# GpSimd operations that wait for the VectorE operation ahead of them, one product split in two, one read moved from PSUM to SBUF, and a new order of the work

## The chip, the cores and the metric

The kernel runs on 1 core of one Trainium2 chip. The metric is the time of one execution on the device in microseconds (us), as the median of several runs. The core has five engines, which take their instructions in order, each from its own queue, and wait for each other by semaphores: TensorE (PE: matmuls; its weight loads are listed as PEld), VectorE (DVE), ScalarE (ACT: table functions such as Sin, Exp and Gelu, and copies), GpSimd (POOL), and SyncE (SP, which here issues DMAs).

## The reference

The input u has 2048 rows of 512 channels. It is normalised, passed through a long convolution whose kernel comes from a diagonal state-space model with 128 complex states for each channel, and added to itself; the result goes through two layernorms and an MLP of width 1376 and is added again. Cut to what matters:

```python
def conv(u):                                   # u: layernorm(x), [1, 2048, 512]
    dt = exp(log_dt)[:, None]
    logdA, dB = dt * (A_re + 1j*A_im), dt * (B_re + 1j*B_im)
    P = exp(logdA[:, :, None] * arange(L))
    K = einsum("dn,dnl,dn->dl", C_re + 1j*C_im, P, dB).real
    y = irfft(rfft(pad(u.T)) * rfft(pad(K)))[:, :L]       # causal, length 2L
    return y.T + u * Dskip

h  = x + conv(layernorm(x))
y  = layernorm(layernorm(h))
h2 = h + gelu(y @ w1 + b1) @ w2 + b2           # w1 512x1376, w2 1376x512
```

Inputs and the output are bf16.

## The kernel before

The kernel computes the convolution through a discrete Fourier transform that is written as matmuls. Its work comes in stages that overlap. First tables: dt, the phases and magnitudes of the states, the coefficients (names gr, gi, t4, den, HLq), small code tables (W2, W3, W4, S4, S2, codT, BD, DD) and the layernorm of the input (`bn_stats`, L913). They are made by DVE and ACT with the help of GpSimd. Parts of the phases are moved between partitions by 32 KB SBUF-to-SBUF DMAs on SP's queue, called restacks here (L541, `ar<-ar`). ACT also takes exponentials (L766).

Then comes the chain. A group of small matmuls (L1032, L1035, L1041) sums phase pieces in PSUM so that the low 16 bits of the result are an angle. ACT takes Sin of those 16 bits (L1050), once for the sine and once for the cosine. DVE multiplies a table of magnitudes with both. There are four such chains, B and A, each for hf=0 and hf=1. In a chain of kind A, and in the second half of a chain of kind B, one DVE operation of 128x2048 (`product`, recorded at L1011) writes the sine and the cosine part at once; in the first half of a B chain they are two operations of 1024 (L1061, L1063) with a negation between (L1062). Another Sin of 128x2048 (name T, L613) belongs to the phases that follow.

From the tables the matmuls of `kgen` (L1090, L1091) and of `kgen4` (L1121, L1122) make the convolution kernel. Four stages (0 to 3) of `kspec` (L1161) take it into frequency space; the stages 0 and 2 belong to the even lines. The result goes to DRAM and back in another layout (K0 and then K1; tiles AK_d), and `fstage` (L958) and `xspec` (L938, L958) finish the transforms of kernel and input. `inverse` multiplies the spectra (DVE, L1201), transforms back (PE, L1211) and transposes by DMA (`turn`, L1217). `tail(b, sb)` adds the residual (PE, L1275 and L1280), takes the statistics (`bn_stats`, L1288), normalises (L1303, L1305) and transposes (PE, L1313). `mlp` is the matmuls L1334 (w1, followed by Gelu on ACT, L1336) and L1356 (w2, followed by DVE, L1358) and the output's DMAs. w1 is loaded in four DMAs of 344 KB, w2 in three.

What sets the order: every operation is recorded with `add` as an entry with the engines it may run on and what it reads and writes. Its dependencies follow from that, by the byte ranges of the tiles. The list `ORDER` at the top names the entries in the order in which they are given out; a negative entry (the bitwise complement of the index) means the second of two engines. A helper `PD`, or `eng="POOL"`, makes an entry that may run on GpSimd or DVE; `CP` and `evac` one that may run on DVE or ACT. `Sched.run` walks the list with a model of costs. This model gives out the four PSUM tiles of 128x1024 f32, and it puts filler matmuls (L1450, results unused) where it expects TensorE to be idle for over 0.6 us; it moves no operation. At the end all operations are issued as listed, each engine's in the order of the list:

```python
    with tc.manual_schedule():
        for o in order:
            o.fn(o.e)
```

A wait is put in where an operation reads or writes bytes that another touches. GpSimd and DVE operations without common data have no order between them.

Of the kernel before, what the change touches and what calls it, by code (L numbers as in the profile page):

```python
# [15 lines left out]
P = 128  # L16
# [143 lines left out]
class VS(V):  # L160
# [93 lines left out]
class Sched:  # L254
# [42 lines left out]
    def run(self, nslots):  # L297
# [7 lines left out]
        slots = [0.0] * nslots  # L305
        taken = [None] * nslots
        dma_busy, bulk = 4.0, 4.0
        ipe, blk, md, pst, issued = 16, 0.0, 0, 0.0, 0.0
        order, seen = [], set()
        assert sorted(i if i >= 0 else ~i for i in ORDER) == list(range(len(ops)))  # L310
        for code in ORDER:
# [14 lines left out]
            if e == "DVE" and dv:  # L326
                s = max(s, pst)
# [75 lines left out]
def kernel(ctx, tc, A_u, A_A_re, A_A_im, A_B_re, A_B_im, A_C_re, A_C_im, A_log_dt, A_Dskip,  # L403
# [1054 lines left out]
    with tc.manual_schedule():  # L1458
        for o in order:
            o.fn(o.e)  # L1460
# [30 lines left out]
```

## Time and profile before

| what | us |
|---|---|
| median of 3 runs | 261.51 |
| lowest and highest run | 260.98, 262.74 |
| the profiled execution's own time | 261.88 |
| its span, first to last instruction | 260.0 |
| GpSimd's work after 43 us | 5.20 of 30.4 |

Times in the profile count from the start of the span. A group of instructions is named by its line in the code, the engine, the operation and what it writes and reads (`ar` is the SBUF arena, `ps` is PSUM), with the number of instructions, the busy time and the mean duration in ns. A row of a timeline gives start, duration and, in brackets, the idle time of the engine just before, with what ended it. Rows of queues end in q (SPq: a DMA issued by SP). The chain that ended last follows the work back from the last instruction, at each step to what released it.

### The profile page before, as it was taken

Reading aid. Unit: us, or ns where it says so; the run is one execution under the profiler, and the core shown is the slowest. Engines: PE = TensorE matmul, PEld = TensorE weight load, DVE = VectorE, ACT = ScalarE, POOL = GpSimd, SP = SyncE. Lnnn points to the kernel's source line nnn. Section 1 sums busy time; section 2 is a strip of 40 time slices with the busy share of each in tenths; the row PEclk is TensorE's granted clock in tenths of the full one; section 3 lists DMA queues with packets and bytes.
Section 4 is the critical chain, followed back from the end, with each engine's and each line's share of the span. In section 5 each row is a group of like instructions: output and inputs, shape, how many; then the busy total and the mean of one; then the engine's idle time right before and its main releaser. Section 6 shows DMA issues by size and latency. Waiting matters only on the chain.

```text
span 260.0 us, 7650 instructions
## 1 busy us (share of the span) xinstructions
PE 222.7 (86%) x3232; PEld 123.2 (47%) x3232; DVE 180.0 (69%) x352; ACT 175.9 (68%) x212; POOL 30.4 (12%) x212
## 2 busy tenths in 40 slices
PE   6307749976978999978999996899999999999994
PEld 2202523332756387423566863665544444444443
DVE  4699999699888858694899858676659962011022
ACT  2899968699978986886899946955620723623610
POOL 8665910070000000000000000000000000000000
PEclk9999995999999999997999999999999999999999
DMA  6981120110040142797476789714071051600302
GB/s 124 186 182 45 39 51 8 36 8 3 3 125 3 33 159 76 243 273 205 118 227 176 156 176 233 202 31 83 9 142 33 20 103 31 141 0 20 73 11 70
DMA packets 43203, 25.06 MB, mean 96 GB/s; under 512 B 27665, under 2 KB 40562, under 8 KB 43170
## 3 DMA queue, kind: packets, MB, share of 16 engines
q1 hardware_dynamic: 42578, 24.13, 38.6%
q10 hardware_dynamic: 592, 0.46, 1.2%
q8 instruction: 25, 0.41, 0.6%
q14 instruction: 8, 0.07, 0.1%
HBM read 10.03 MB, written 6.29 MB: 63 GB/s over the span
## 4 chain that ended last, share of the span: by engine, by line
PE 51%; ACT 15%; DMA 14%; DVE 10%; issue 4%; SPq 4%; ACTq 0%; DVEq 0%
PE ps L1334 15%; PE ps L1356 15%; ACT ar L529 7%; ACT ar L1050 6%; PE ps L1211 5%; DMA ar<-in_A_u_dram 5%; DMA ar<-ar 4%; SPq L541 3%; DMA ar<-AK_d 3%; PE ps L1450 3%; DMA AK_d<-ar 2%; DVE ar L606 2%; PE ps L1041 2%; DVE ar L1011 2%; PE ps L958 2%
## 5 line engine op out<-in xcount | busy, mean ns | idle before, releaser
L529 ACT CAST ar<-ps 128x1024 bf16<-128x1024 f32 (+4 forms) x74 | 66.7, 977 | 17.3 <-DVE ar L1288 5.9
L1336 ACT ACTIVATE ar<-ps,ar 128x512 bf16<-128x512 f32 (+1 forms) x44 | 28.8, 684 | 37.6 <-PE ps L1334 24.0
L1334 PE MATMUL ps<-ar 128*128 128x512 bf16 (+1 forms) x176 | 40.0, 379 | 0.0
L1356 PE MATMUL ps<-ar 128*128 128x512 bf16 (+3 forms) x187 | 39.9, 367 | 0.0
L1358 DVE TENSOR_TENSOR ar<-ps,ar 128x512 bf16<-128x512 f32 (+1 forms) x17 | 11.1, 659 | 40.4 <-PE ps L1356 29.8
L1050 ACT ACTIVATE ar<-ps 128x1024 bf16<-128x1024 int16 x36 | 34.9, 1053 | 4.1 <-PE ps L1041 2.8
L1201 DVE TENSOR_TENSOR ar<-ar 128x1024 bf16<-128x1024 bf16 x48 | 30.3, 686 | 10.2 <-PE ps L1211 9.7
L531 DVE CAST ar<-ps 128x1024 bf16<-128x1024 f32 (+3 forms) x26 | 28.5, 1116 | 9.4 <-PE ps L958 4.9
L1041 PE MATMUL ps<-ar 128*32 128x512 f16 (+1 forms) x368 | 23.5, 348 | 6.9 <-ACT ar L1050 3.7
L1356 PEld LDWEIGHTS <-ar 128*128 128x128 bf16 (+1 forms) x187 | 18.1, 98 | 20.0 <-issue 0.4
L1334 PEld LDWEIGHTS <-ar 128*128 128x128 bf16 (+1 forms) x176 | 17.4, 100 | 20.0
L1211 PE MATMUL ps<-ar 64*128 64x128 bf16 x768 | 24.0, 216 | 0.9 <-ACT ar L529 0.5
L1211 PEld LDWEIGHTS <-ar 64*128 64x128 bf16 x768 | 21.6, 94 | 6.3 <-DVE ar L1201 2.7
L1011 DVE TENSOR_TENSOR ar<-ar 128x2048 bf16<-128x2048 bf16 x18 | 21.7, 1222 | 3.1 <-PE ps L1091 2.6
L958 PE MATMUL ps<-ar 128*32 128x512 bf16 (+1 forms) x320 | 19.2, 363 | 4.9 <-ACT ar L529 2.4
L1450 PE MATMUL ps<-ar 128*128 128x512 bf16 x57 | 17.2, 450 | 5.7 <-DMA ar<-in_A_u_dram 5.1
L1041 PEld LDWEIGHTS <-ar 128*32 128x32 f16 x368 | 10.5, 101 | 17.7 <-issue 15.4
L613 ACT ACTIVATE ar<-ar 128x512 f32<-128x512 f32 (+9 forms) x19 | 12.6, 694 | 6.8 <-DVE ar L606 3.5
L766 ACT ACTIVATE ar<-ar 128x1024 bf16<-128x1024 f32 x16 | 15.7, 1042 | 0.8 <-DVE ar L600 0.8
L938 PE MATMUL ps<-ar 128*32 128x512 bf16 x256 | 15.4, 380 | 0.0
L606 DVE SCALAR_TENSOR_TENSOR ar<-ar 128x4 f32<-128x4 f32 (+4 forms) x44 | 13.3, 308 | 1.3 <-ACT ar L613 0.4
L958 PEld LDWEIGHTS <-ar 128*32 128x32 bf16 x320 | 8.2, 100 | 12.3 <-issue 6.4
(107 smaller groups left out, 281.0 us busy)
## 6 DMA issues: line engine op xcount, KB each, us to landing
ar<-AK_d SPq DMA_DIRECT2D x8, 512.0 KB
ar<-in_A_u_dram SPq DMA_DIRECT2D x4, 512.0 KB, 11.3
AK_d<-ar SPq DMA_DIRECT2D x2, 1024.0 KB
AK_d<-ar SPq DMA_DIRECT2D x4, 512.0 KB
out_dram<-ar SPq DMA_DIRECT2D x30, 64.0 KB, 2.0
ar<-in_B_w_dram SPq DMA_DIRECT2D x4, 344.0 KB, 6.8
ar<-ar SPq DMA_DIRECT2D x40, 32.0 KB, 1.8
ar<-in_B_w_dram SPq DMA_DIRECT2D x2, 640.0 KB
```

Of the source, the lines that this page charges most:

```text
L529: act.copy(out_fn(), in_fn())
L531: dve.tensor_copy(out_fn(), in_fn())
L958: pe.matmul(pst(p)[64 * h + z:64 * h + z + 32, w * (k + r):w * (k + r) + w], lhsT=T.ap()[:, f, r, z:z + 32], rhs=v[f:f + 1].ap()[:, 0, :], ...
L1011: dve.tensor_tensor(o, E_(o).unsqueeze(1).to_broadcast(shape), f, ALU.mult)
L1041: pe.matmul(pst(p)[32 * g:32 * g + 32, 256 * j:256 * (j + n)].rearrange("p (a b) -> p a b", a=n), lhsT=W2[DELTAS.index(d)].ap(), rhs=S2[g] ...
L1050: add("ACT", c_act(1024), lambda e, o_=o_, i_=i_: act.activation(o_(), i_(), ACT.Sin, scale=SINSC), r=[p, TBL], w=[sc[cs]])
L1201: dve.tensor_tensor(o, a, b_[:, :, ::-1, :] if sw else b_, ALU.mult)
L1211: pe.matmul(pst(p)[:, 512 * h + 128 * k:512 * h + 128 * k + 128], lhsT=q.ap()[rows, 2 * k + r, :], rhs=TP[w].ap()[rows, f0 // 2 + k, :], s ...
L1334: pe.matmul(pst(p)[:fs, 512 * z:512 * z + 512], lhsT=w1s[dc].ap()[:, fc * P:fc * P + fs], rhs=ybuf.ap().rearrange("p (t c) k -> p c t k", ...
L1336: add("ACT", c_act(512, 1), lambda e, p=p, z=z, fc=fc, fs=fs: act.activation(hT.ap()[:fs, fc, :], pst(p)[:fs, 512 * z:512 * z + 512], ACT. ...
L1356: pe.matmul(pst(p)[:, 512 * z + c0:512 * z + c1], lhsT=hT.ap()[:fs, fc, 128 * t:128 * t + 128], rhs=w2s[fc].ap()[:fs, c0:c1], start=(fc == ...
L1450: pe.matmul(slots[z][:, 0:512], lhsT=identb.ap(), rhs=hs[15].ap(), start=True, stop=True)
```

## The change

It has six parts.

1. `ORDER` is replaced by another list. Among the engines chosen by it: the product that makes W3 (128x640) and two memsets go from DVE to GpSimd; the product that makes W2, one conversion of 1024 for codT, the four conversions for DD (128x32) and one memset go from GpSimd to DVE; two conversions (th and the first half of HLq) go from DVE to ACT. The Sin of 128x2048 is listed during `kgen4`, not after the first two Sin of the chain. The kspec stages 0 and 2 come after the chain's last product, not ahead of it; the first 17 of 24 halves of `kgen4` precede all of `kspec`. 12 of the 16 pieces of the second `xspec` are listed ahead of the return of K0. The load of A_im stands second among SP's first loads, not behind two loads of u; the loads of u lie later, between restacks; that of B_re is issued on ACT's queue behind the one of log_dt. All four loads of w1 stand behind the fifth DMA transpose.
2. Every operation on GpSimd that is not a DMA waits for the last DVE instruction ahead of it in the list. `Sched.run` models this as `held`.
3. In the B chain with hf=1 the product of 2048 is written as two of 1024 (four products become eight).
4. The two copies of one transposed PSUM tile, crt (512, ACT) and cit (512, DVE), become one of 1024 on ACT.
5. In `tail(0, 0)` the copy from PSUM comes first, and `bn_stats` reads the copy.
6. The model's constants change: the first loads cost 1.25 times as much, a carry 0.75 and 57,344 B, a load of the spectrum 0.7, and fillers are put in from an idle time of 0.4 us on. There are 79 filler matmuls in place of 57; the other 3175 matmuls are the same in number.

Line numbers behind the changed parts are 4 to 15 higher in the kernel after (L1011 becomes L1015, L1050 becomes L1054, L1201 becomes L1209, L1450 becomes L1458).

```diff
 ORDER = [
-    182, 15, 0, 1, 12, 13, 16, 2, 311, 3, 5, 154, 17, 43, 37, 65, 66, 156, 18, 19, 4, 11, 20, 147, 36, 8, 67, 68, 21, 22, 23, 42, 44, 64, 45, 47, 57,
+    0, 1, 13, 143, 6, 2, 79, 12, 15, 144, 155, 3, 43, 110, 153, 11, 42, 80, 181, 4, -155, 32, 45, 5, 9, 44, -48, 16, 17, 59, 46, 14, 139, 65, 66, 60,
...
@@ Sched.run
+            if e == "POOL" and o.byts == 0:
+                s = max(s, held)
...
-            if e == "PE" and self.src <= seen and s - free[e] > 0.6 and fs:
+            if e == "PE" and self.src <= seen and s - free[e] > 0.4 and fs:
...
-                while t + (0.3 if clk.warm and clk.end > t else 0.55) < s and n0 < FILLN:
+                while t + (0.2 if clk.warm and clk.end > t else 0.4) < s and n0 < FILLN:
...
+            if e == "DVE":
+                held = end + LAG["DVE"]
...
-    crt, cit = tE(bf16, 512), tE(bf16, 512)
-    evac(by4(crt), pas[0], 512, [p], [crt])
-    evac(by4(cit), pas[1], 512, [p], [cit], pr=0.401)
+    cc = tE(bf16, 2, 512)
+    crt, cit = cc[0], cc[1]
+    evac(lambda: cc.ap().rearrange("p z (q d) -> p z q d", d=4), lambda p=p: pst(p, bf16)[:, 0:1024].rearrange("p (z d q) -> p z q d", z=2, d=4), 1024, [p], [cc])
...
             rE, rI = regs(e0, q, lo, 4), regs(i0, q, lo, 4)
+            if hf:
+                add("DVE", c_dve(1024, 2), lambda e, lo=lo, Sx=Sx, e0=e0, i0=i0, q=q: dve.tensor_tensor(ent(i0, q, lo, 4), ent(e0, q, lo, 4), Sx(), ALU.mult), r=rE + [sc[0]], w=rI)
+                add("DVE", c_dve(1024, 2), lambda e, lo=lo, Cx=Cx, e0=e0, q=q: dve.tensor_tensor(ent(e0, q, lo, 4), ent(e0, q, lo, 4), Cx(), ALU.mult), r=rE + [sc[1]], w=rE + mark)
+                continue
             product(lambda e0=e0, q=q, lo=lo: both(e0, q, lo, 4), lambda o: o[:, 1], sc, rE + [sc], rE + rI + mark)
...
-                add("DVE", c_dve(512, 1, True) + 0.05, lambda e, src=src, j=j, hh=hh: dve.bn_stats(st2[8 * b + j].ap(), src() if first else hh.ap()), r=[p if first else hh], w=[st2[8 * b + j]], hv=0)
-                if first:
+                else:
                     evac(lambda hh=hh: hh.ap(), src, 512, [p], [hh])
+                add("DVE", c_dve(512) + 0.05, lambda e, j=j, hh=hh: dve.bn_stats(st2[8 * b + j].ap(), hh.ap()), r=[hh], w=[st2[8 * b + j]], hv=0)
...
     with tc.manual_schedule():
+        held, last = nc.cur_bb.bb.instructions, None
         for o in order:
+            n0 = len(held)
             o.fn(o.e)
+            if o.e == "DVE":
+                last = held[-1].name
+            elif o.e == "POOL" and o.byts == 0 and last is not None:
+                tc.add_manual_dep(held[n0], last, mybir.DependencyInfo(mybir.DependencyClass.Sync, mybir.DependencyReason.DATA), reason="turns")
```

More of the change, by code (lines that the diff above doesn't have):

```diff
@@ L307, in run @@
         dma_busy, bulk = 4.0, 4.0
-        ipe, blk, md, pst, issued = 16, 0.0, 0, 0.0, 0.0
+        ipe, blk, md, pst, issued, held = 16, 0.0, 0, 0.0, 0.0, 0.0
         order, seen = [], set()
@@ L621 @@
         raw[nm] = tE(bf16, 4, P)
-        dma(("SP", "ACT", "SP", "ACT", "SP", "SP")[n], lambda v=raw[nm]: v.ap(), lambda a=ap: a.rearrange("(p dt) n -> p dt n", dt=4), 131072, [], [raw[nm]], pr=0.01 * n)
+        dma(("SP", "ACT", "SP", "ACT", "SP", "SP")[n], lambda v=raw[nm]: v.ap(), lambda a=ap: a.rearrange("(p dt) n -> p dt n", dt=4), 131072, [], [raw[nm]], pr=0.01 * n, k=1.25)
         if n == 0:
             ldt = tE(bf16, 512)
-            dma("ACT", lambda: ldt.ap(), lambda: A_log_dt.partition_broadcast(P), 131072, [], [ldt], pr=0)
+            dma("ACT", lambda: ldt.ap(), lambda: A_log_dt.partition_broadcast(P), 131072, [], [ldt], pr=0, k=1.25)
     xv = x_dram.rearrange("(b q j h l) d -> b h q j (l d)", b=2, j=4, h=2, l=2)
@@ L630 @@
             half = xb.part(64 * h, 64 * h + 64)
-            dma("SP", lambda half=half: half.ap(), lambda b=b, h=h: xv[b, h], 524288, [], [half], pr=0.1)
+            dma("SP", lambda half=half: half.ap(), lambda b=b, h=h: xv[b, h], 524288, [], [half], pr=0.1, k=1.25)
     S.pr = 0.1
@@ L1138, in fn @@
                 nc.sync.dma_start(a[32 * g + NA:32 * g + 32, 0:32], a[32 * g + NA - CY:32 * g + 32 - CY, 1:33])
-            add("SP", 0.55, fn, r=[kg], w=[("carry", q)], byts=49152 * (1 + q), pr=pr)
+            add("SP", 0.75, fn, r=[kg], w=[("carry", q)], byts=57344 * (1 + q), pr=pr)
     def kspec(b, q, pr, ak, nb, n):
@@ L1178, in kstage @@
             n = 8 // nb
-            dma("SP", lambda fh=fh, n=n: kf[n * fh:n * fh + n].ap(), lambda fh=fh, n=n: D.rearrange("s (q f) d -> (s q) f d", f=16)[:, n * fh:n * fh + n, :], 524288, [("AK", bs, q, 0), ("AK", bs, q, 1)], [kf[n * fh:n * fh + n], ("KFR", q, bs, fh)], k=0.65)
+            dma("SP", lambda fh=fh, n=n: kf[n * fh:n * fh + n].ap(), lambda fh=fh, n=n: D.rearrange("s (q f) d -> (s q) f d", f=16)[:, n * fh:n * fh + n, :], 524288, [("AK", bs, q, 0), ("AK", bs, q, 1)], [kf[n * fh:n * fh + n], ("KFR", q, bs, fh)], k=0.7)
         fstage(kf, 2 * nb)
```

68 rows, old and new, of the table ORDER are left out of this document.

## The prediction

> **What bounds the kernel now.** I read the page first (busy time, slices, chain), then a table by stage, then the timelines of the stages in which the change works.
>
> ```profile
> PE 222.7 (86%) x3232; PEld 123.2 (47%) x3232; DVE 180.0 (69%) x352; ACT 175.9 (68%) x212; POOL 30.4 (12%) x212
> PE 51%; ACT 15%; DMA 14%; DVE 10%; issue 4%; SPq 4%; ACTq 0%; DVEq 0%
> ```
>
> TensorE carries 51% of the chain, but 49% is others' work. The table by stage (us, then the busy time of PE, PEld, DVE, ACT, POOL, then clock, DMA share, GB/s) says where:
>
> ```profile
> 0.00:43.00 43.00, 23.40 (x247) 11.33 (x247) 36.67 (x83) 33.17 (x40) 25.23 (x207) 0.96 0.49 96
> 43.00:90.00 47.00, 39.75 (x940) 22.31 (x938) 40.50 (x64) 42.37 (x49) 5.20 (x5) 0.96 0.13 29
> 90.00:130.00 40.00, 37.02 (x610) 21.58 (x608) 29.01 (x40) 32.54 (x37) 0.00 (x0) 0.96 0.58 174
> 130.00:170.00 40.00, 36.21 (x854) 24.98 (x847) 32.57 (x62) 33.08 (x38) 0.00 (x0) 1.00 0.80 194
> 170.00:260.00 90.00, 86.35 (x605) 43.01 (x599) 41.28 (x105) 34.74 (x51) 0.00 (x0) 1.00 0.26 53
> ```
>
> Until 43 us tables are made, mostly by DVE and ACT, and GpSimd's work nearly all lies there; until 90 the chain of Sin and products, again ACT and DVE; from 130 TensorE leads. The last 90 us are TensorE's (86.35 of 90), and nothing of the change makes its work less. So what is gained must be gained before 90 us and survive the way to 170.
>
> **Stage 1: GpSimd's turns.** DVE, start and duration in us (a row x2 is two instructions), then GpSimd:
>
> ```profile
> 10.67 0.62 DVE L606 SCALAR_TENSOR_TENSOR ar<-ar 128x512 f16<-128x512 f32 x1
> 20.72 0.43 DVE L600 TENSOR_SCALAR ar<-ar 128x512 f16<-128x512 f32 x1
> 24.37 3.01 DVE L600 TENSOR_SCALAR ar<-ar 128x512 f16<-128x512 f32 x2
> 27.30 1.15 DVE L606 SCALAR_TENSOR_TENSOR ar<-ar 128x512 f16<-128x512 f32 x1
> 30.37 1.17 DVE L606 SCALAR_TENSOR_TENSOR ar<-ar 128x512 f16<-128x512 f32 x1
> ...
> 23.97 1.37 POOL L1387 TENSOR_TENSOR ar<-ar 128x512 f32<-128x512 f32 x1
> 25.31 1.79 POOL L590 TENSOR_TENSOR ar<-ar 128x672 f32<-128x672 f32 x1
> 32.01 1.27 POOL L590 TENSOR_TENSOR ar<-ar 128x512 f32<-128x512 f32 x1
> ```
>
> The same instruction takes 0.62 us alone and 1.15 and 1.17 beside GpSimd; two of 0.43 took 3.01 while two GpSimd products ran. That is 2.15 + 0.53 + 0.55 = 3.2 us lost in these rows. The change makes each GpSimd operation wait for the DVE operation ahead of it in the list. The Trainium skill, page "SBUF — State Buffer", section "Who interferes with whom", says that GpSimd and a DVE instruction with two SBUF inputs, or in a two-port mode, exclude each other for a whole instruction, and that issue order decides who waits. By that rule the loss only changes hands: an operation let go when DVE is done meets DVE's next one, and either blocks the other. The rows above agree that the DVE instruction waits out a whole GpSimd one; none shows the other order. I take between nothing and 3.2 us off DVE, nearer 3.2, since the next DVE instruction is already queued when the GpSimd one is still being told.
>
> How much of it reaches the first Sin? ACT, then PE and SP:
>
> ```profile
> 39.92 0.31 ACT L613 ACTIVATE ar<-ar 128x16 f32<-128x16 f32 x1 [3.50 <-DVE ar L606]
> 42.56 0.63 ACT L613 ACTIVATE ar<-ar 128x512 f32<-128x512 f32 x1
> 43.09 1.92 ACT L1050 ACTIVATE ar<-ps 128x1024 bf16<-128x1024 int16 x2
> 44.90 1.91 ACT L613 ACTIVATE ar<-ar 128x2048 bf16<-128x2048 int16 x1
> 48.87 1.94 ACT L1050 ACTIVATE ar<-ps 128x1024 bf16<-128x1024 int16 x2 [2.05 <-PE ps L1041]
> ...
> 18.11 20.30 SPq L541 DMA_DIRECT2D ar<-ar  x26
> 44.50 3.77 PE L1450 MATMUL ps<-ar 128*128 128x512 bf16 x12
> ```
>
> ACT waits 3.50 us for the layernorm statistics, then goes through the square root, a table load and the first two Sin at 43.09. With DVE earlier and the statistics pulled forward in the list, that wait goes. What is late next is ACT itself: two conversions of 512 move to it from DVE (two of 0.63 by the 42.56 row), and one copy out of PSUM grows from 512 to 1024, which I put at up to another 0.63. Net 3.50 − 1.26 − 0.63 = 1.6; for waits on the loads at the start, in a new order, I keep 0.3 back: the first Sin at 43.09 − 1.3 = 41.8. Bounds: 0 (the 26 restacks, SP busy to 38.4, hold TensorE's first chain group) and 3.5. On DVE the moves about cancel: a 128x512 product, a conversion of 1024 and four of 128x32 come from GpSimd; a product of 128x640, two conversions and the copy go. The other edits of this stage are list order and the planner's constants; A_im's load, moved ahead of the u loads, and B_re's, now on ACT's queue, are hidden behind ACT, which is busy from the start; uncovered they would cost one issue each (0.54 by the row of a w1 load below).
>
> **Stage 2: the chain of products.** The Sin of 128x2048 (1.91 us) no longer follows the first two chain Sins; it comes in the later kernel-generation part, beside TensorE work. But the next pair at 48.87 was held by PE: 12 filler matmuls took 3.77 us (I read them as planned to fit the gap and overrun). After, ten fillers stand there, so of 1.91 I count 0.7 (bounds 0 and 1.9). That makes −2.0 at the end of the first two chains.
>
> Then the false waits:
>
> ```profile
> 74.45 1.23 DVE L1011 TENSOR_TENSOR ar<-ar 128x2048 bf16<-128x2048 bf16 x1 [1.18 <-PE ps L1091]
> 75.71 1.05 ACT L1050 ACTIVATE ar<-ps 128x1024 bf16<-128x1024 int16 x1 [1.23 <-DVE ar L1011]
> DVE ar L1011 <- PE ps L1091: 2.6, 3, 1.2
> L1063 DVE TENSOR_TENSOR ar<-ar 128x1024 bf16<-128x1024 bf16 x8 | 5.5, 687 | 0.0
> 89.29 1.22 DVE L1011 TENSOR_TENSOR ar<-ar 128x2048 bf16<-128x2048 bf16 x1 [0.33 <-ACT ar L1050]
> ```
>
> The 2048-wide product writes sine and cosine halves in one; its whole range waits for matmuls L1091 that read an earlier part. Split in two of 1024, it waits for DVE alone. Gone: 2.6 us of DVE and 1.23 of ACT behind it, together 3.8. Added: four products become eight, 4 × (2 × 0.687 − 1.22) = 0.6 by mean durations; instructions overlap at their ends, so I count nothing and keep 0.6 as the bound. What is late next is DVE, nearly without a gap, and TensorE's kernel matmuls, which were waiting for the same products. So the last product of the chain, done at 89.29 + 1.22 = 90.5, is done at 90.5 − 2.0 − 3.8 = 84.7.
>
> **What is handed on.** Two stages of kernel spectrum, 32 matmuls, ran before that point and now come after:
>
> ```profile
> 87.87 1.25 PE L1161 MATMUL ps<-ar 20*128 20x512 bf16 x18
> 89.31 1.04 PE L1161 MATMUL ps<-ar 20*128 20x512 bf16 x14 [0.19 <-ACT ar L1050]
> ```
>
> 1.25 + 1.04 = 2.3 us go back behind it. In return part of the input's spectrum comes earlier (12 of 16 pieces before the K0 data land, most of them after before), which fills the wait for the round trip through DRAM:
>
> ```profile
> 101.78 5.50 DMA AK_d<-ar
> ...
> 109.22 8.54 DMA ar<-AK_d
> 117.79 4.06 PE ps L958 x40
> ```
>
> For that and for the new order of this part I count nothing, and shift all behind by 5.8 − 2.3 = 3.5 us: K0's first matmuls at about 117.79 − 3.5 = 114.3.
>
> **The PSUM read in tail(0,0).** Here ACT's copies out of PSUM stood behind DVE's statistics, which read the same tile:
>
> ```profile
> 158.47 7.69 ACT L529 CAST ar<-ps 128x512 bf16<-128x512 f32 x10 [5.88 <-DVE ar L1288]
> 160.03 0.62 PE L958 MATMUL ps<-ar 128*32 128x256 bf16 x16 [1.78 <-ACT ar L529]
> ...
> 150.40 2.76 PE L1450 MATMUL ps<-ar 128*128 128x512 bf16 x12
> ```
>
> Now the copies come first and DVE reads the copy in SBUF. ACT can start when the matmuls are done, some 2 us sooner, and PE's wait of 1.78 goes. What is late next are the statistics, now behind four copies, and then the transposes before the MLP: there the list has 14 fillers where it had 3 and 1. Twelve took 2.76 us, so ten more are 2.3 us that run whether needed or not. Bounds: 1.78 gained, 2.3 − 1.78 = 0.5 lost; I take 1.0 gained, since TensorE waits for the statistics there in any case and part of the fillers falls into that wait. The first MLP comes at 170.42 − 3.5 − 1.0 = 165.9 (its row is below). Behind it lie 89.6 us of TensorE's work, as before: the end is at 255.5.
>
> The span is 255.5 against 260.0. The profiled run took 261.88 by itself, 1.88 over its span; the median of the runs shown is 261.51, 1.51 over it. With 1.51: **257.0**.
>
> **Rivals.** More gain: after 90 us TensorE idles 170 − (37.02 + 36.21 + 86.35) = 10.4 us by the table. If the new order fills 2 to 5 us of it, most around the wait for K0, 252 to 255. For: the input's spectrum is there for that. Against: those waits end with DMAs, whose durations don't change.
>
> Gain eaten: the Sin of 1.91 and the spectrum stages now stand ahead of K0's store, and the fillers ahead of the transposes run blind. If the Sin comes back in full and the 1.0 of tail(0,0) is not to be had, 257.0 + 1.9 + 1.0 = 259.9, and with the 2.3 us of fillers on top 262.2: no change.
>
> Slower, by the loads of w1. Before, the second of four was issued at 112.74; now all four stand on SP's queue behind the fifth DMA transpose:
>
> ```profile
> 112.74 0.54 SPq L541 DMA_DIRECT2D ar<-in_B_w_dram  x1
> 153.40 5.94 SPq L1217 DMA_TRANSPOSE ar<-ar  x1
> ar<-in_B_w_dram SPq DMA_DIRECT2D x4, 344.0 KB, 6.8
> 170.42 3.63 PE L1334 MATMUL ps<-ar 128*128 128x512 bf16 x16
> ```
>
> SP comes free of that transpose at 159.3, in shifted time 155.8. Four loads side by side land at 155.8 + 4 × 0.54 + 6.8 = 164.8, just before the first MLP at 165.9; one after another, 155.8 + 4 × 6.8 = 183.0. From 165.9 on every us counts in full; past 173.0 (257.0 + 7.1 = 264.1) the kernel is over 1% slower, and at 183.0 the time is 274. For: that stretch moves most (share 0.80, 194 GB/s). Against: 4 × 344 KB = 1.4 MB at 194 GB/s is 7.3 us, so landed at 163.1, if nothing else moves.
>
> GpSimd late: its last product ended at 33.28, and 11 operations that read SBUF now wait for DVE. Up to 41.8 there are at most 8.5 us of slack, 0.77 per operation; at 1.42 each, some two DVE products, the first Sin is 7.1 us late and the time 264. This is how the skill's rule of the shared pair would turn against the change. If instead the stalls stay with DVE, the first Sin stays at 43.1 and the time is 258.3.
>
> **How the numbers follow.** The measured runs lie within 0.7% of each other; under 1% (below 258.9 to above 264.1 are the bounds) counts as no change. Forecast as worked out, 255.5 to 259.5: 0.44, of it 0.33 below 258.9 and 0.11 above. More gain, 252 to 255.5: 0.17. Gain eaten, 259.5 to 262.5: 0.16. w1 late, 264 to 274: 0.12. GpSimd late, 264 to 267: 0.11. Faster 0.33 + 0.17 = 0.50, the same 0.11 + 0.16 = 0.27, slower 0.23. The range 253 to 265 leaves out a third of the second case, most of w1's and half of GpSimd's, together about 0.2. The likeliest sign by itself, faster, has 252 to 258.9.
>
> **What would show it.** In the profile after: DVE's f16 products in stage 1 all near 0.62 and the L600 pairs near 0.43 each; no 3.50 us wait of ACT for the statistics; first chain Sin near 41.8; the split products without a PE wait; last chain product done near 84.7; K0's first matmuls near 114.3; no 5.88 us wait of ACT for statistics before the MLP, whose first matmuls come near 165.9 with no wait for w1. I am wrong if the first Sin is not before 43, if the 5.8 us are there at 85 and gone at 118 (gain eaten), or if the first MLP's weights wait for a DMA.

## The result and the profile after

The kernel after takes 251.57 us in the median of 4 runs (251.25 to 252.43); the kernel before, on the same chip, 261.38 (260.98 to 262.74). The ratio is 0.9621 with a 95% interval of 0.9579 to 0.9663. The profiled execution took 251.55 us by itself, 1.75 over its span of 249.8. The forecast was 257.0 with a range of 253 to 265: the sign was right, and the gain was twice what was forecast. Runs of one kernel differ (over all experiments those of before lie between 257.92 and 263.39 us, those of after between 250.17 and 254.02), and a profile shows one of them.

The page of the kernel after, busy time and the chain that ended last:

```profile
PE 223.2 (89%) x3240; PEld 123.9 (50%) x3254; DVE 175.5 (70%) x355; ACT 176.6 (71%) x216; POOL 24.1 (10%) x208
PE 61%; ACT 23%; DVE 9%; issue 4%; POOL 0%; DVEq 0%; ACTq 0%; POOLq 0%
```

TensorE's work is the same (223.2 us, before 222.7), in a shorter span. DMA and SyncE's queue, together 18% of the chain of before, are gone from it, and ScalarE has 23% in place of 15%.

Four points of the two profiles show where the 10.2 us of span come from:

| point in the profile | before | after | gained so far |
|---|---|---|---|
| first Sin of the chain | 43.09 | 39.19 | 3.9 |
| last product of the chain done | 90.5 | 80.5 | 10.0 |
| first matmul of the MLP | 170.42 | 159.83 | 10.6 |
| end of the span | 260.0 | 249.8 | 10.2 |

Nearly all of it is there at the chain's last product. From there to the end, the sums of two tables of windows (first before, then after; span, then busy times):

```profile
sum 169.50, PE 159.23 PEld 89.58 DVE 102.37 ACT 99.86 POOL 0.00; mean PE 39.81 PEld 22.39 DVE 25.59 ACT 24.96 POOL 0.00
```

```profile
sum 169.30, PE 161.64 PEld 90.24 DVE 103.04 ACT 102.70 POOL 0.52; mean PE 40.41 PEld 22.56 DVE 25.76 ACT 25.67 POOL 0.13
```

The same length: TensorE has 2.4 us more to do there (in the main 2.3 for the two spectrum stages that were handed on and 2.2 for more fillers, less 1.7 that 40 matmuls of before lost to a slow clock, see the last section), and does it in time that was idle before. Its waits ahead of the L958 matmuls (L962 after) fall from 4.9 to 0.9 us; 2.1 of them were for the load of AK_d, for which it no longer waits.

Stage 1 after, ScalarE first, then VectorE, then GpSimd, in rows of the timeline (start, duration, idle time ahead):

```profile
6.66 0.63 ACT L602 ACTIVATE ar<-ar 128x512 f32<-128x512 f32 x1 [1.38 <-DVE ar L594]
7.32 4.84 ACT L770 ACTIVATE ar<-ar 128x1024 bf16<-128x1024 f32 x5
12.07 0.99 ACT L533 COPY ar<-ps 128x1024 bf16<-128x1024 bf16 x1
37.23 1.28 ACT L527 ACT_TABLE_LOAD   x1
39.19 1.00 ACT L1054 ACTIVATE ar<-ps 128x1024 bf16<-128x1024 int16 x1
...
8.45 0.69 DVE L610 SCALAR_TENSOR_TENSOR ar<-ar 128x512 f16<-128x512 f32 x1
20.66 0.69 DVE L594 TENSOR_TENSOR ar<-ar 128x512 f16<-128x512 f32 x1
27.67 4.83 DVE L917 BATCH_NORM_STATS2 ar<-ar 128x6 f32<-128x512 bf16 x8
...
22.72 1.25 POOL L718 TENSOR_TENSOR ar<-ar 128x640 f16<-128x640 f32 x1
24.14 0.90 POOL L584 TENSOR_SCALAR ar<-ar 128x8 f32<-128x8 int32 x1
27.93 1.27 POOL L594 TENSOR_TENSOR ar<-ar 128x512 f32<-128x512 f32 x1 [1.51 <-ACT ar L770]
32.13 0.67 POOL L584 TENSOR_SCALAR ar<-ar 128x512 int32<-128x512 f32 x1
```

ScalarE works from 6.66 to the table load at 37.23 almost without a gap; its wait of 3.50 us is gone. The products on VectorE take 0.69 us, none takes 1.15, and GpSimd's last larger operation ends at 32.8, with no delay against before (33.28). From 21.49 us on GpSimd's larger operations run beside VectorE's statistics, and these take no longer for it: eight in 4.83 us, as in the experiment a_no_turns below, where GpSimd is idle during most of the same eight.

The chain, and the part ahead of the MLP (VectorE, ScalarE, SyncE, PE):

```profile
43.21 1.29 DVE L1065 TENSOR_TENSOR ar<-ar 128x1024 bf16<-128x1024 bf16 x2
79.28 1.22 DVE L1015 TENSOR_TENSOR ar<-ar 128x2048 bf16<-128x2048 bf16 x1 [0.53 <-ACT ar L1054]
...
84.69 1.96 ACT L617 ACTIVATE ar<-ar 128x2048 bf16<-128x2048 int16 x1
147.39 1.07 ACT L533 CAST ar<-ps 128x512 bf16<-128x512 f32 x2 [3.54 <-PE ps L1288]
...
148.08 2.49 SPq L545 DMA_DIRECT2D ar<-in_B_w_dram  x5
...
148.60 1.06 PE L962 MATMUL ps<-ar 128*32 128x256 bf16 x32
153.20 3.20 PE L1458 MATMUL ps<-ar 128*128 128x512 bf16 x13
159.83 5.35 PE L1342 MATMUL ps<-ar 128*128 128x512 bf16 x24
```

From the first product to the end of the last the chain takes 37.3 us (before 43.4). The copies of tail(0,0) wait for matmuls, not for the statistics. The loads of w1 are issued from 148.08, and the first MLP matmuls come at 159.83 with no wait ahead of them: w1 is there in time.

### The profile page after: what moved, and what is told of

Read it like the earlier page. It is cut to its first block, busy times and chain, and to the rows that moved or that the text cites. A ratio compares the mean times of both kernels' runs of the same rounds, so it can differ in the third digit from the quotient of the medians.

```text
span 249.8 us, 7666 instructions
## 1 busy us (share of the span) xinstructions
PE 223.2 (89%) x3240; PEld 123.9 (50%) x3254; DVE 175.5 (70%) x355; ACT 176.6 (71%) x216; POOL 24.1 (10%) x208
## 4 chain that ended last, share of the span: by engine, by line
PE 61%; ACT 23%; DVE 9%; issue 4%; POOL 0%; DVEq 0%; ACTq 0%; POOLq 0%
PE ps L1342 15%; PE ps L1364 15%; PE ps L1219 8%; ACT ar L770 6%; ACT ar L1054 6%; ACT ar L533 5%; PE ps L942 4%; PE ps L1169 3%; PE ps L1288 2%; PE ps L1458 2%; DVE ar L1015 2%; ACT ar L617 2%; PE ps L962 2%; PE ps L1129 2%; ACT ar L995 2%
## 5 line engine op out<-in xcount | busy, mean ns | idle before, releaser
L533 ACT CAST ar<-ps 128x1024 bf16<-128x1024 f32 (+3 forms) x75 | 66.6, 972 | 17.3 <-PE ps L1219 5.7
L1344 ACT ACTIVATE ar<-ps,ar 128x512 bf16<-128x512 f32 (+1 forms) x44 | 28.0, 686 | 35.2 <-PE ps L1342 27.7
L1209 DVE TENSOR_TENSOR ar<-ar 128x1024 bf16<-128x1024 bf16 x48 | 30.1, 686 | 10.3 <-PE ps L1219 9.8
L1054 ACT ACTIVATE ar<-ps 128x1024 bf16<-128x1024 int16 x36 | 34.5, 1041 | 1.9 <-PE ps L1045 1.6
L535 DVE CAST ar<-ps 128x1024 bf16<-128x1024 f32 (+2 forms) x25 | 28.2, 1148 | 9.3 <-ACT ar L533 3.9
L1045 PE MATMUL ps<-ar 128*32 128x256 f16 (+1 forms) x368 | 21.5, 331 | 4.2 <-ACT ar L1054 3.8
L1458 PE MATMUL ps<-ar 128*128 128x512 bf16 x72 | 20.9, 421 | 4.8 <-DMA ar<-in_A_u_dram 4.2
L962 PE MATMUL ps<-ar 128*32 128x512 bf16 (+1 forms) x320 | 17.5, 338 | 0.9 <-ACT ar L533 0.6
L1015 DVE TENSOR_TENSOR ar<-ar 128x2048 bf16<-128x2048 bf16 x14 | 16.9, 1230 | 1.1 <-ACT ar L1054 1.1
L1045 PEld LDWEIGHTS <-ar 128*32 128x32 f16 x368 | 9.5, 96 | 14.6 <-issue 11.7
L1458 PEld LDWEIGHTS <-ar 128*128 128x128 bf16 x79 | 7.7, 105 | 16.1 <-issue 10.5
L988 PE MATMUL ps<-ar 128*32 128x256 f16 x160 | 8.0, 337 | 5.0 <-POOL ar L718 3.1
```

Of the source, the lines that this page charges most:

```text
L533: act.copy(out_fn(), in_fn())
L535: dve.tensor_copy(out_fn(), in_fn())
L1045: pe.matmul(pst(p)[32 * g:32 * g + 32, 256 * j:256 * (j + n)].rearrange("p (a b) -> p a b", a=n), lhsT=W2[DELTAS.index(d)].ap(), rhs=S2[g] ...
L1054: add("ACT", c_act(1024), lambda e, o_=o_, i_=i_: act.activation(o_(), i_(), ACT.Sin, scale=SINSC), r=[p, TBL], w=[sc[cs]])
L1209: dve.tensor_tensor(o, a, b_[:, :, ::-1, :] if sw else b_, ALU.mult)
L1344: add("ACT", c_act(512, 1), lambda e, p=p, z=z, fc=fc, fs=fs: act.activation(hT.ap()[:fs, fc, :], pst(p)[:fs, 512 * z:512 * z + 512], ACT. ...
```

## The experiments

Names with a_ are made from the kernel after, with one part undone; names with b_ from the kernel before, with one part added. Where entries of the list are moved, the fillers and the PSUM tiles are held at those of the kernel that it was made from. Line numbers in these kernels are 4 or 5 higher. The ratio is to the kernel before, run on the same chip, with its 95% interval. The last columns are points of the profile, in us.

| kernel | median us | ratio | first Sin | last product done |
|---|---|---|---|---|
| after | 251.57 | 0.962 (0.958 to 0.966) | 39.19 | 80.50 |
| a_no_turns | 252.59 | 0.966 (0.961 to 0.971) | 40.37 | 81.86 |
| a_loads_old | 255.06 | 0.976 (0.970 to 0.983) | 42.59 | 84.08 |
| a_u_early | 251.25 | 0.963 (0.958 to 0.969) | 39.18 | 80.29 |
| a_no_split | 254.92 | 0.977 (0.973 to 0.981) | 39.19 | 84.14 |
| a_t_early | 253.65 | 0.973 (0.968 to 0.978) | 39.18 | 82.26 |
| a_tail_old | 255.46 | 0.981 (0.975 to 0.987) | 39.19 | 81.25 |
| a_no_fill | 253.19 | 0.971 (0.965 to 0.977) | 39.19 | 82.60 |
| a_no_late_fill | 251.17 | 0.963 (0.957 to 0.968) | 39.18 | 80.96 |
| after_again | 250.99 | 0.960 (0.954 to 0.967) | 39.19 | 80.52 |
| a_no_late_fill_2 | 250.84 | 0.960 (0.955 to 0.966) | 39.19 | 81.13 |
| a_order_alone | 265.10 | 1.016 (1.011 to 1.022) | 43.54 | 90.71 |
| b_turns | 259.19 | 0.989 (0.982 to 0.996) | 41.40 | 86.78 |
| b_loads_new | 259.98 | 0.993 (0.990 to 0.997) | 42.25 | 87.67 |
| b_split | 258.47 | 0.993 (0.989 to 0.997) | 42.18 | 87.39 |
| b_t_late | 262.18 | 1.003 (0.999 to 1.007) | 41.74 | 88.68 |
| b_tail | 260.05 | 0.997 (0.993 to 1.000) | 42.66 | 88.11 |
| b_loads_turns | 259.49 | 0.991 (0.987 to 0.994) | | |
| b_all_parts | 260.70 | 0.997 (0.993 to 1.001) | 42.18 | 86.98 |

The points come from one execution each: its own time lies 1.5 to 1.6 us below the median for b_turns, b_t_late and b_all_parts, and 3.7 us above it for b_loads_turns, whose points are left out. b_split, b_t_late and b_tail have the first stage of before unchanged, and their first Sin lies at 41.7 to 42.7, where the profile of before shows 43.09: points of b_ kernels are known to about 1 us. The scatter follows the landing of log_dt, for which ScalarE's first operation waits: that operation starts at 4.70, 5.50, 5.98 and 6.42 us in b_t_late, b_split, b_tail and before, and the first Sin comes 36.7 to 37.0 us later in each.

### Turns and loads, each undone

```diff
-            elif o.e == "POOL" and o.byts == 0 and last is not None:
+            elif False:
```

> The kernel after, without the waits of GpSimd on VectorE; the list, the fillers and the PSUM tiles are the same. Theory A (the turns gave the early start): products on VectorE take up to 1.2 us and more beside GpSimd again, the first chain Sin comes at 41 to 43 in place of 39.2, and the time is 253.5 to 255.5. Theory B (the order of the first loads gave it, the turns little): the first Sin within 0.7 us of 39.2 and the time within 1 us of 251.6.

The entries of SyncE's first loads in the order of the list (6 is A_im, 7 to 10 are the loads of u); the entries between them are left out, and in a_loads_old all of these but 8 stand ahead of the first restack:

```diff
-    0, 6, 3, 5, 9, 10, 7, 8,
+    0, 3, 5, 9, 10, 6, 7, 8,
```

> The kernel after, with SyncE's first loads in the manner of before: two loads of u go ahead of A_im, and the third right behind it. Theory B: ScalarE's wait for log_dt and TensorE's wait for A_im come back, the first chain Sin is 2.5 to 4 us later than 39.2, and the time is 254 to 256. Theory A: ScalarE's other work hides it, the first Sin moves by less than 1 us and the time stays within 1 us of 251.6.

Without the turns 1.0 us is lost (252.59 against 251.57), and the first Sin comes 1.2 us later. VectorE in a_no_turns:

```profile
21.66 1.76 DVE L594 TENSOR_TENSOR ar<-ar 128x512 f16<-128x512 f32 x1
```

The product that takes 0.69 in the kernel after takes 1.76 here, beside a GpSimd product: the stalls are what the turns remove. Two more stand ahead of it: conversions that take 1.88 and 2.20 us in place of 0.20 and 0.95, each beside a memset of GpSimd. With the old loads 3.5 us are lost (255.06), and the first Sin comes 3.4 us later. TensorE and ScalarE in a_loads_old:

```profile
12.26 0.61 PE L755 MATMUL ps<-ar 128*128 128x128 bf16 x4 [6.72 <-DMA ar<-in_A_A_im_dram]
...
14.61 1.01 ACT L538 COPY ar<-ps 128x1024 bf16<-128x1024 bf16 x1 [2.45 <-PE ps L789]
```

TensorE waits 6.72 us for A_im to transpose it, the transposes behind it wait too, and ScalarE's copy comes at 14.61, where it came at 12.07. A_im's load is issued at 4.67 us here, at 1.20 in the kernel after. The first exponential starts at 7.32 in both, and ScalarE has no slack left to absorb what follows. So in the new list the loads (theory B) carry most of the early start, the turns (theory A) a smaller part.

### The same two, added to the kernel before

b_turns adds the seven lines of the change that make the waits, b_loads_new moves three entries of the old list (SyncE's entries in order; 88 to 95 are restacks):

```diff
-    0, 3, 5, 8, 7, 6, 9, 92, 89, 94, 95, 88, 93, 10,
+    0, 6, 3, 5, 8, 92, 89, 7, 94, 95, 88, 9, 93, 10,
```

> The kernel before, with the waits of GpSimd on VectorE added and nothing else. Theory A: VectorE's stalls of some 3 us go, ScalarE's wait of 3.5 us for the statistics shrinks, and the time is 258 to 260. Theory B: the loads set the start, the time is 260.5 to 262. If the waits need a list that is made for them, GpSimd comes late: 262 to 265.

> The kernel before, with A_im loaded second and the second and third load of u put between the restacks, and nothing else. Theory B: TensorE's wait of 4.7 us for A_im goes, ScalarE starts 1 to 2 us earlier, and the time is 258 to 260. Theory A: the same time as before, within 1 us of 261.4, since the statistics stay late.

> The kernel before, with the new place of the loads and with the turns, the list otherwise as it was. If the two add up (1.5 and 2.2 us alone): 257 to 258, first chain Sin at about 40.5. If they need each other (the loads free VectorE early, the turns keep it free): 255 to 256.5, first Sin near 39.2. If they share one gain: 258.5 to 259.5.

They win 1.1% and 0.7%, and together 0.9% (0.6 to 1.3%): they do not add up, and the expectation of the third kernel that holds is that they share one gain, of some 2 us, though it lies at the upper end. GpSimd and ScalarE in b_turns show what the old list loses with the turns:

```profile
39.55 1.28 POOL L590 TENSOR_TENSOR ar<-ar 128x512 f32<-128x512 f32 x1
...
27.50 0.72 ACT L613 ACTIVATE ar<-ar 128x512 f32<-128x512 f32 x1 [1.41 <-POOL ar L590]
40.87 0.63 ACT L613 ACTIVATE ar<-ar 128x512 f32<-128x512 f32 x1 [0.44 <-POOL ar L590]
41.40 1.92 ACT L1050 ACTIVATE ar<-ps 128x1024 bf16<-128x1024 int16 x2
```

GpSimd's last product, made at 32.01 before, is now made at 39.55, because its operations stand behind VectorE's statistics in that list. ScalarE no longer waits 3.50 us for the statistics, but twice for GpSimd, 1.41 and 0.44 us. So the mechanism of the rival "GpSimd late" is there, at a smaller price: the kernel is still faster than before. The new list has these operations further ahead.

### Which of the loads

In a_u_early entries 3, 5, 9, 10 and 7 stand directly behind 6 in the list, with no restack (the entries from 87 on) between them:

> The kernel after, with three loads of u directly behind the five small loads of SyncE, A_im still second. If the place of A_im counts: within 0.7 us of 251.3. If the u loads in flight slow the small ones, or the restacks behind them: 253 to 255.

```diff
-    0, 6, 3, 5, 9, 88, 91, 10, 93, 87, 89, 7,
+    0, 6, 3, 5, 9, 10, 7, 88, 91, 93, 87, 89,
```

251.25 us, the first Sin at 39.18: nothing is lost. Three loads of 512 KB in flight early do no harm; what counts is that A_im stands ahead of them.

### The split and the long Sin

```diff
-                add("DVE", c_dve(1024, 2), lambda e, lo=lo, Sx=Sx, e0=e0, i0=i0, q=q: dve.tensor_tensor(ent(i0, q, lo, 4), ent(e0, q, lo, 4), Sx(), ALU.mult), r=rE + [sc[0]], w=rI)
-                add("DVE", c_dve(1024, 2), lambda e, lo=lo, Cx=Cx, e0=e0, q=q: dve.tensor_tensor(ent(e0, q, lo, 4), ent(e0, q, lo, 4), Cx(), ALU.mult), r=rE + [sc[1]], w=rE + mark)
-                continue
+                add("DVE", 0.0, lambda e: None, r=rE + [sc[0]], w=rI)
             product(lambda e0=e0, q=q, lo=lo: both(e0, q, lo, 4), lambda o: o[:, 1], sc, rE + [sc], rE + rI + mark)
```

> The kernel after, with the products of the second B chain as one instruction of 2048 again; two of these products stand one place earlier in the list, because the sine half alone no longer frees its tile. Theory C (the prediction's: the false waits are worth 3.8 us on the path): waits of VectorE for the kernel matmuls L1099 come back, the chain's last product ends at 83 to 84.5 in place of 80.5, and the time is 254.5 to 256. Rival (the new order has moved the kernel matmuls out of the way, the split does little): the last product by 81.5, the time within 1 us of 251.6.

The last product is done 3.6 us later and the time is 3.35 us longer. Two rows of VectorE and the waits of a_no_split:

```profile
70.04 1.22 DVE L1020 TENSOR_TENSOR ar<-ar 128x2048 bf16<-128x2048 bf16 x1 [1.23 <-PE ps L1102]
82.91 1.23 DVE L1020 TENSOR_TENSOR ar<-ar 128x2048 bf16<-128x2048 bf16 x1 [0.53 <-ACT ar L1059]
```

```profile
ACT ar L1059 <- DVE ar L1020: 3.5, 3, 2.2
DVE ar L1020 <- PE ps L1102: 2.3, 2, 1.2
```

The rows of waits give the total, the number and the longest, in us. The false waits are back, VectorE's for the kernel matmuls and ScalarE's behind it; the kernel after has neither. Theory C holds.

> The kernel before, with each product of the second B chain as two instructions of 1024, one right behind the other. Theory C: VectorE's waits for L1091 (2.6 us) and ScalarE's behind it (1.2 us) go, the last product ends 3 to 4 us earlier than 90.5 and the time is 257.5 to 259. Rival (another wait takes its place): 260.5 to 261.5.

In b_split one entry of the list makes both halves, one right behind the other; the list is the same. It wins 0.7%, about 1.9 us by the ratio, half of what was expected. VectorE's waits for the kernel matmuls are gone there too. Why the old list makes less of it is not shown; the halves keep the place of the whole in it.

The long Sin, moved in the list from its place in the `kgen4` part to behind the second chain Sin (entry 300 behind 249), and in the kernel before the other way (entry 301 behind 464):

```diff
-    -229, 297, 249, 242,
+    -229, 297, 249, 300, 242,
...
-    457, 463, 300, 317,
+    457, 463, 317,
```

> The kernel after, with the Sin of 128x2048 behind the first two Sin of the chain, where it stood before. If it costs its whole duration on the path (ScalarE is the bound of the chain): the last product 1.9 us later, the time 253 to 254. The prediction's 0.7: 252 to 252.7. If VectorE is the bound and the Sin falls into its idle time: within 0.4 us of 251.6.

> The kernel before, with the Sin of 128x2048 among the later kernel matmuls, as in the kernel after; the fillers stay where they are. If the 12 fillers behind it are the bound there, little is won: 260.8 to 261.5. If the whole 1.9 us counts: 259 to 260.

In the new list it costs 2.1 us, its whole duration and a little more; in the old list its going wins nothing that can be measured. ScalarE and VectorE in a_t_early, then ScalarE in b_t_late:

```profile
43.09 1.90 ACT L622 ACTIVATE ar<-ar 128x2048 bf16<-128x2048 int16 x1
...
46.85 0.69 DVE L1070 TENSOR_TENSOR ar<-ar 128x1024 bf16<-128x1024 bf16 x1 [2.02 <-ACT ar L1059]
...
47.40 1.94 ACT L1054 ACTIVATE ar<-ps 128x1024 bf16<-128x1024 int16 x2 [3.74 <-PE ps L1045]
```

VectorE waits 2.02 us for the chain Sin behind the long one. The 12 fillers that held TensorE there in the kernel before have fewer successors in the new list (9, 2, 7 and 3 in four places), so the wait for the Sin is the last one to end. In b_t_late the fillers are still there, and ScalarE's wait for TensorE grows from 2.05 to 3.74 us: it takes up most of the 1.91 us that the Sin leaves free.

### The PSUM read

```diff
-                else:
-                    evac(lambda hh=hh: hh.ap(), src, 512, [p], [hh])
-                add("DVE", c_dve(512) + 0.05, lambda e, j=j, hh=hh: dve.bn_stats(st2[8 * b + j].ap(), hh.ap()), r=[hh], w=[st2[8 * b + j]], hv=0)
+                add("DVE", c_dve(512, 1, True) + 0.05, lambda e, src=src, j=j, hh=hh: dve.bn_stats(st2[8 * b + j].ap(), src() if first else hh.ap()), r=[p if first else hh], w=[st2[8 * b + j]], hv=0)
+                if first:
+                    evac(lambda hh=hh: hh.ap(), src, 512, [p], [hh])
```

The eight entries change places in the list accordingly, the statistics of a tile ahead of its copies. b_tail is the same edit the other way in the kernel before.

> The kernel after, with tail(0,0) as before: the statistics read the tile in PSUM and come ahead of ScalarE's copies. The prediction's 1.0 us for this edit: 252.6. If the whole wait of TensorE counts: 253.4. If the statistics themselves set the way to the MLP, in either order: 251.6, and the 14 fillers ahead of the transposes hide it.

> The kernel before, with ScalarE's copies ahead of the statistics in tail(0,0), which then read the copies. 1.0 to 1.8 us faster than before if the copies' wait of 5.9 us is on the path; the same as before (260.5 to 261.5) if the statistics are.

3.9 us in the new list, more than any expectation had; 0.3% (0 to 0.7%) in the old one. ScalarE, TensorE and one window (length, busy times of PE, PEld, DVE, ACT and POOL, granted clock, DMA share, GB/s) of a_tail_old:

```profile
150.91 3.19 ACT L538 CAST ar<-ps 128x512 bf16<-128x512 f32 x5 [6.80 <-DVE ar L1301]
...
152.03 1.04 PE L967 MATMUL ps<-ar 128*32 128x256 bf16 x16 [2.56 <-ACT ar L538]
154.20 3.60 PE L1224 MATMUL ps<-ar 64*128 64x128 bf16 x64
...
151.00:157.00 6.00, 4.82 (x86) 3.94 (x87) 3.30 (x17) 4.90 (x7) 0.00 (x0) 0.55 0.92 320
```

TensorE waits 2.56 us for the copies, and behind the wait its clock is granted at 0.55: 16 matmuls take 1.04 us where 16 took 0.62 at 148.85 in the same profile, and 64 take 3.60 where 64 took 1.96. In this execution the wait and the slow clock make the loss: the first MLP matmul comes at 165.24, 5.4 us later than in the kernel after, with 2.6 us of waiting and 2.8 us by the clock (0.42 twice, 1.64, and 0.32 in four more matmuls). This execution took 257.05 us, the other three 254.87 to 255.53, so the median loss of 3.9 us lies between the wait alone and the two together; how much of the slow clock the other three had, no trace shows. In the kernel before the wait was 1.78 us, and the same 16 matmuls behind it took 0.62: there the clock held.

### The fillers

> The kernel after, without any of the 79 filler matmuls. If they only cost time where the waits turn out shorter than planned: 1 to 3 us faster, 248.5 to 250.5. If they keep TensorE's clock up: the granted clock falls below 0.9 in windows behind its waits and the time is 252.5 to 256.

```diff
-                while t + (0.2 if clk.warm and clk.end > t else 0.4) < s and n0 < FILLN:
+                while n0 < FILLS.get(o.i, 0):
```

with an empty table FILLS for a_no_fill and 52 of the 79 fillers in it for a_no_late_fill.

> The kernel after, without the 27 fillers between the convolution's kernel and the MLP (3, 10 and 14 of them); the 52 others stay. If these delay the transposes ahead of the MLP: 0.5 to 2 us faster. If the waits are as long as planned: the same within 0.5 us. If the clock falls for them: slower by up to 2 us.

Without any fillers 1.6 us are lost, and the window from 40 to 50 us shows it, first in a_no_fill, then in the kernel after:

```profile
40.00:50.00 10.00, 7.21 (x75) 2.23 (x68) 9.57 (x19) 7.91 (x12) 0.00 (x0) 0.69 0.10 26
```

```profile
40.00:50.00 10.00, 9.79 (x109) 3.56 (x113) 9.86 (x19) 8.49 (x12) 0.00 (x0) 1.00 0.10 26
```

The granted clock is 0.69 in place of 1.00, and the last product is done 2.1 us later. The 27 late fillers were left out in two experiments, the second on the same chip as the kernel after:

> The kernel after, unchanged, as the measure for the next one: 251 to 252.5.

> The kernel after without the 27 late fillers, on the same chip as the kernel after. If fillers that outlast their wait delay the transposes: 0.5 to 1.5 us faster than the kernel after. If not: within 0.4 us of it.

250.84 against 250.99: they cost nothing and win nothing.

### All parts in the old list, and the new list without them

b_all_parts has the turns, the new loads, the split (as in b_split), the late long Sin and the new tail in the kernel before. a_order_alone has all five undone in the kernel after; what stays of the change is the rest of the list, the one copy of crt and cit, and the fillers.

> The kernel before, with the loads, the turns, the split, the late long Sin and the new tail; the rest of the list, the fillers and the single copy of crt and cit stay as before. If the parts make the gain: 251 to 253.5. If half of it belongs to the rest of the new order: 254 to 257.

> The kernel after, with the old place of the loads, no turns, the products of 2048, the long Sin early and the old tail, all at once; what is left of the change is the rest of the new order, the single copy of crt and cit, and the fillers. If the parts add up as each cost by itself (3.5 + 1.0 + 3.4 + 2.1 + 3.9 = 13.9): 265. If the rest of the order keeps a gain of its own: 257 to 260. If they overlap so that none is left: 260.5 to 262.5.

In the old list the five parts together win nothing that can be measured (0.997, 0.993 to 1.001). The new list without them is 1.6% slower than before (1.1 to 2.2%). The five losses by themselves, 1.0 + 3.5 + 3.35 + 2.1 + 3.9, sum to 13.9 us, and 251.57 + 13.9 = 265.4, where 265.10 was measured: in the new list they add up. Up to the last product a_order_alone is where the kernel before is (90.71 and 90.5); it loses most of its 4.5 us in the stretch up to the MLP, whose first Gelu starts at 175.15 (before 171.50), the stretch of the tail with the old read.

ScalarE in b_all_parts, ahead of the chain:

```profile
8.35 3.90 ACT L770 ACTIVATE ar<-ar 128x1024 bf16<-128x1024 f32 x4 [1.86 <-DVE ar L604]
28.25 0.72 ACT L617 ACTIVATE ar<-ar 128x512 f32<-128x512 f32 x1 [1.41 <-POOL ar L594]
41.65 0.63 ACT L617 ACTIVATE ar<-ar 128x512 f32<-128x512 f32 x1 [0.47 <-POOL ar L594]
```

A_im is early here too, but the first Exp still starts at 8.35 (after: 7.32), since VectorE's list makes its input late, and ScalarE waits twice for GpSimd.

## Why the prediction was wrong

The span was forecast at 255.5 and came to 249.8. Of the 5.7 us between them 2.6 are missed at the first Sin (41.8 forecast, 39.19), 1.6 on the way to the chain's last product (84.7 and 80.5), and 1.9 from there to the MLP (165.9 and 159.83); the MLP itself takes 0.4 longer. The largest miss is the first.

**The first Sin: −1.3 forecast, −3.9 measured.** The step that failed is the sum 3.50 − 1.26 − 0.63 − 0.3. ScalarE before:

```profile
6.42 1.29 ACT L613 ACTIVATE ar<-ar 128x512 bf16<-128x512 bf16 x2 [2.98 <-DMA ar<-in_A_log_dt_dram]
8.55 3.90 ACT L766 ACTIVATE ar<-ar 128x1024 bf16<-128x1024 f32 x4 [0.84 <-DVE ar L600]
```

The sum held ScalarE's start fixed, but its first exponential comes 1.23 us earlier, at 7.32 in place of 8.55. From there to the first Sin its idle time falls from 3.83 us to none, where 3.50 were taken, and its work grows by 1.15 us (30.71 to 31.86), where 1.26 + 0.63 = 1.9 were taken; the 0.3 kept back was not needed. 1.23 + 3.83 − 1.15 = 3.9. Part of the 1.23 is luck: it hangs on when log_dt lands, and kernels with the first stage of before show the first Sin up to 1.35 us earlier than the profile that the sum started from. In nine profiles of kernels that start as the kernel after does, ScalarE's first operation starts at 4.52 to 4.93, and the first exponential waits for VectorE instead; which of the moved loads does that, no run separates.

The sentence on A_im's load, "hidden behind ACT, which is busy from the start; uncovered they would cost one issue each", failed too, though in the new list alone. In the kernel before the load was hidden: TensorE waited 4.7 us for it, and ScalarE's copy at 12.35 did not. In the new list A_im's transposes stand ahead of that copy, and the old place of the load would cost 3.4 us at the first Sin and 3.5 us of time (a_loads_old). So its new place prevents a loss that the new list would bring, and by itself, in the old list, it wins 0.7% (b_loads_new).

**The turns.** That the stalls of VectorE go was right; the reason given, that its next instruction is queued before GpSimd is told, no run shows. VectorE's products take 0.69, and GpSimd's three 128x512 products of f32 1.04 to 1.27 (before 1.27 to 1.37). The Trainium skill, page "SBUF — State Buffer", section "Who interferes with whom", has the order of issue decide who waits. In the kernel after hardly anyone waits: the list and the turns put GpSimd's larger operations beside the statistics, which take no longer for it, and one small conversion of GpSimd pays (0.90 us at 24.14, beside a product; 0.40 in a_no_turns). The turns are worth 1.0 us, a third of the 3.2 us that VectorE lost. In the old list they win 1.1% and make GpSimd late, as the rival had it, though the time does not grow.

**The long Sin: 0.7 taken, 2.1 measured.** The bound of 1.9 was nearly it. I took the value nearer to the fillers of before, of which fewer stand there in the new list; in the old list, with them, it is worth nothing (b_t_late).

**The split: 3.8 taken, 3.35 measured.** Right, mechanism and size, in the new list; in the old one it wins 1.9.

**The two handed-on spectrum stages: +2.3 taken, nothing measured.** From the last product to the end it is 169.3 us, 0.2 less than before, though TensorE is busy 2.4 us longer. The idle time there took them up, above all that ahead of the L958 matmuls and for AK_d. The prediction had named the reason (12 of 16 pieces of `xspec` ahead of K0's return) and priced it at nothing; no run undoes it by itself.

**The PSUM read: 1.0 taken, 0.9 (0 to 1.8) measured in the old list and 3.9 in the new one.** For the list that the sum started from the price was right. In the new list the wait is longer, 2.56 us in place of 1.78, and the slow clock that can follow it was not priced. The rival in which the ten more fillers eat the gain is refuted: without the 27 late ones the time is the same.

**The rest of the change: nothing taken; by itself it costs 4.5 us** (265.10 against 260.65 on the same chip). It is paid back by the five parts, which in the old list win next to nothing. Summing edits against the profile of before priced them in a list that no longer exists. That the sum came out too small, not too large, is due to the parts being worth more in the new list: 13.9 − 4.5 = 9.4, where 9.8 us were won.

**The rivals.** More gain had 0.17 and, at 252 to 255.5, came nearest with its fast end; its mechanism, idle time behind the chain that is filled, is right only for the 2.3 us above. w1 late did not happen (first MLP matmul with no wait). Gain eaten did not happen: 10.0 us at the last product, 10.6 at the MLP.

On one point the section on the change misleads: B_re's load was issued on ScalarE's queue before, too, at 1.67 us. What changes is that it now follows ScalarE's first operation, at 4.65.

What stays open: which moves in the rest of the list cost the 4.5 us, most of it in the stretch ahead of the MLP, and why log_dt lands earlier and more evenly with the new loads.

## What to carry to other kernels

An engine that seems to have slack because it waits in one place late has none once that wait is removed: then each small delay at its start counts in full, here the place of one 128 KB load. An edit's price is a property of the list it stands in: the same five edits win nothing measurable in one order and are worth 14 us in another, so a new order and its edits have to be tried together, and undone one by one. A wait of TensorE costs its length and, in some executions, a slow clock behind it.

## What was not expected of the hardware

TensorE's clock can fall behind waits of about 2 us, and the length of the wait does not decide it. Waits in one profiled execution each, and what the clock did behind them:

| wait of TensorE | us | clock granted behind it | matmuls behind it, us |
|---|---|---|---|
| before, in tail(0,0) | 1.78 | 1.00 | 16 in 0.62 |
| a_no_late_fill, for VectorE | 1.93 | 1.00 | 64 in 1.96 |
| a_no_late_fill_2 (the same kernel), same place | 1.93 | 0.50 for 3.4 us | 64 in 3.58 |
| before, for AK_d | 2.10 | 0.50 for 3.4 us | 40 in 4.03 |
| b_loads_new and b_tail, for AK_d | 2.13, 2.14 | 0.50 for 3.4 us | 40 in 4.00, 3.99 |
| b_split, for AK_d | 2.17 | 1.00 | 40 in 2.35 |
| b_t_late, for AK_d | 2.38 | 1.00 | 40 in 2.35 |
| a_tail_old, in tail(0,0) | 2.56 | 0.55 in 151 to 157 us | 16 in 1.04, 64 in 3.60 |

The Trainium skill, page "TensorE: Matmul & The Clock Gate", section "Part 1: The HAM clock gate", has the clock fall after at least one idle window of about 3.4 us that runs free. All these waits were shorter, and ahead of that of a_tail_old TensorE was busy without a gap from 146 us on; the measurement decides. In the kernel after TensorE does not wait for AK_d, so this loss, 1.7 us in the profile of before, is gone with the wait.

The first stage of the kernel after repeats to 0.01 us: the first Sin at 39.18 or 39.19 in nine profiles, a_u_early with other places for the loads of u among them. That of the kernel before scatters from 41.74 to 43.09 in four, with the landing of log_dt.
